# Batch left-over rows through SyncE and a GpSimd cast, a shared buffer (hbuf) in two tiles, and an earlier reorder in an attention and MLP kernel

## The chip, the cores and the metric

One core of one Trainium2 chip. The time is the device time of one execution in microseconds (us); a kernel's figure is the median of its runs. A profiled execution also has a span, from its first to its last instruction, which is about 2 us shorter than the time. In the profile PE is TensorE's matmuls, DVE VectorE, ACT ScalarE, POOL GpSimd, SP SyncE; L233 is a line of the kernel. The granted clock is TensorE's clock as a share of its full speed. The changed kernel has more lines, so the same statement has another number: L233 before is L260 after, L270 is L297, L364 is L391, L401 is L428.

## The reference

```python
def _attn_ref(q, k, v):                       # 8 batches, 12 heads, 448 rows, 64 columns, fp32
    scores = scale * np.matmul(q, k.transpose(0, 1, 3, 2))
    m = np.max(scores, axis=-1, keepdims=True)
    e = np.exp(scores - m)
    attn = e / (np.sum(e, axis=-1, keepdims=True) + np.exp(-m) + 1e-09)
    return np.matmul(attn, v)
def _moe_ref(x, w_in, w_out):                 # x: 3584 x 768; w_in 768 x 2048; w_out 2048 x 768
    h = x @ w_in
    g = 0.5 * h * (1.0 + erf(h * inv_sqrt2))
    return g @ w_out
```

The heads of the attention output are joined to rows of 768, which are x.

## The kernel before

It runs batch by batch in steps of one pair of heads (48 steps, counted from 0). While batch b's MLP runs on TensorE, the scores, exponentials and values of batch b+1 are threaded through it. 448 rows are three blocks of 128 and 64 left-over rows, which are loaded apart (klraw, vl). All inputs are fp32 in memory and fp16 on the chip; the loads on GpSimd's queue cast on the way. From batch 2 on, q and k are transposed by DMA on SyncE's queue, out of a copy in which VectorE has put the heads in pairs (order_by_pairs).

```python
    # after the six start steps of batch 0; all on GpSimd's queue, in this order
    nc.vector.memset(kl_raw[0], 0.0)
    load_q(2, 0, half); load_k(2, 0, half)
    for i in range(2):
        load_w_out(0, i, 2)            # first half of w_out's columns, in two quarters
    load_left(kl_raw, k, 2)            # 4 DMAs of 24 KB
    load_left(vl, v, 1)                # 4 DMAs of 24 KB
    load_v(1, 0, half); load_v(1, half, H)
    for i in range(2):
        load_w_out(1, i, 2)            # second half of w_out's columns
    load_q(2, half, H); load_k(2, half, H)
    ... (cut)
    def fetch_half(b, i):              # batch 2's q and k, three pairs at a time
        c0 = i * NPAIR // 2
        for w in range(2):
            order_by_pairs(b, w, c0, c0 + NPAIR // 2)      # VectorE, into the tile hbuf
            transpose_on_dma(b, w, c0, c0 + NPAIR // 2)    # SyncE
    ... (cut: half 0 is fetched after step 7, half 1 inside step 12)
    def step(s, work, late=False, then=None):
        ... (cut: scores(s), values of older pairs, normalize)
        if then:
            then()                     # where half 1 is fetched
        add_up(...)                    # VectorE: the sums of step s-1, for its denominators
        ... (cut: the MLP's tiles; in their midst denominators(s-1) on TensorE)
```

In the compiled program a load on GpSimd's queue waits for the load eight before it. hbuf is also the tile into which VectorE copies the first-layer results of a batch before their GELU.

The softmax here doesn't subtract the row's maximum and nothing guards it: scores larger than these inputs give would overflow.

## Time and profile before

414.1 us (413.2 to 415.6, 4 runs).

| What | Value | How to read it |
|---|---|---|
| span | 410.9 us | the profiled execution |
| PE busy | 396.3 us, 96% | the bound; no idle time of PE after 92 us |
| PE idle, step 11 | 1.55 us | waits for the last quarter of w_out, until 72.12 |
| PE idle, batch 1's first layer | 0.54 us | waits for a PSUM bank, which waits for hbuf |
| second half of batch 2's k | issued 58.58, landed 75.7 | the last load that VectorE's reorder needs |

### The profile page before, as it was taken

What the parts mean: (1) busy time and instruction counts of PE and PEld (TensorE: products, weight loads), DVE (VectorE), ACT (ScalarE), POOL (GpSimd) and SP (SyncE); (2) the same over time, 40 slices, a digit from 0 to 9 for tenths busy, and PEclk for the clock granted to TensorE, in tenths of its full rate; (3) what the DMA queues carried; (4) which work ended last, traced back from release to release, by engine and by line L of the source; (5) the groups of instructions that cost most, each with busy time, mean ns of one, the idle gap of its engine ahead of it and who ended that gap; (6) DMA issues with size and microseconds to landing.
All of it is one profiled execution on the core that took longest, in us unless ns stands there. A gap on an engine that the chain in (4) does not pass through costs nothing.

```text
span 410.9 us, 10968 instructions
## 1 busy us (share of the span) xinstructions
PE 396.3 (96%) x4679; PEld 245.0 (60%) x4679; DVE 199.8 (49%) x479; ACT 299.6 (73%) x450; POOL 121.1 (29%) x169
## 2 busy tenths in 40 slices
PE   7788998999999999999999999999999999999996
PEld 3444865656656665666666666565566665566663
DVE  5786346773366604673256813576146732530021
ACT  6998889879797847988687856989588766634300
POOL 8751271495732480055500672030000000000000
PEclk9999999999999999999999999999999999999999
DMA  9999999999994992289922999149011010110032
GB/s 160 144 194 203 201 171 217 194 169 160 146 116 106 143 181 35 60 121 139 128 59 59 166 146 86 51 102 151 19 41 58 22 40 2 60 53 9 2 82 73
DMA packets 137185, 43.81 MB, mean 107 GB/s; under 512 B 118256, under 2 KB 137136, under 8 KB 137136
## 3 DMA queue, kind: packets, MB, share of 16 engines
q0 software_dynamic: 91952, 22.39, 58.0%
q1 hardware_dynamic: 44400, 20.10, 26.1%
q8 instruction: 36, 0.59, 0.6%
q10 hardware_dynamic: 784, 0.62, 0.6%
q14 instruction: 13, 0.11, 0.1%
HBM read 45.61 MB, written 11.01 MB: 138 GB/s over the span
## 4 chain that ended last, share of the span: by engine, by line
PE 81%; DMA 14%; POOL 3%; issue 1%; DVE 1%
PE bank L233 65%; DMA w_out_sb<-in_moe_w_out_dram 10%; PE st L330 6%; PE bank L379 6%; DMA rawk<-in_k_dram 4%; PE st L401 2%; PE st L233 2%; PE bank L394 1%; POOL vn L97 1%; POOL rawq L97 1%; PE st L379 1%; POOL vl L129 0%; POOL klraw L129 0%; POOL rawk L97 0%; DVE klraw L177 0%
## 5 line engine op out<-in xcount | busy, mean ns | idle before, releaser
L233 PE MATMUL bank<-xt,w_in_sb 128*64 128x448 f16 x1536 | 151.9, 353 | 0.5 <-DVE hbuf L445 0.5
L318 ACT ACTIVATE et<-st,expb 128x896 f16<-128x896 f32 x144 | 134.3, 1003 | 22.8 <-PE st L330 22.6
L233 PEld LDWEIGHTS <-w_in_sb 128*64 128x64 f16 x1536 | 93.5, 110 | 54.5 <-issue 3.8
L233 PE MATMUL bank<-w_out_sb,gt_odd 128*64 128x384 f16 x1024 | 88.0, 326 | 0.0
L482 DVE COPY osb<-bank 128x384 f32<-128x384 f32 x56 | 31.2, 557 | 103.2 <-PE bank L233 103.1
L233 PEld LDWEIGHTS <-gt_odd 128*64 128x64 f16 x1024 | 57.8, 110 | 27.6 <-issue 2.1
L233 PE MATMUL bank<-w_out_sb,gt_even 128*64 128x384 f16 x768 | 68.5, 327 | 1.5 <-DMA w_out_sb<-in_moe_w_out_dram 1.5
L417 DVE TENSOR_TENSOR xt<-bank,rec 128x448 f16<-128x448 f32 x44 | 27.5, 624 | 76.1 <-PE bank L394 63.5
L233 PEld LDWEIGHTS <-gt_even 128*64 128x64 f16 x768 | 43.2, 110 | 23.8 <-issue 4.9
L441 ACT ACTIVATE gt_odd<-bank 128x448 f16<-128x448 f32 (+1 forms) x74 | 29.2, 394 | 21.3 <-PE bank L233 20.2
L330 PE MATMUL st<-tqk 64*64 64x448 f16 x576 | 41.6, 358 | 2.5 <-ACT et L318 1.5
L113 POOL DMA_DIRECT2D rawq<-in_q_dram x40 | 30.6, 772 | 30.2 <-DMA vn<-in_v_dram 20.7
L318 ACT ACTIVATE el<-st,expb 128x448 f16<-128x448 f32 x48 | 30.7, 640 | 11.1 <-PE st L401 10.4
L445 DVE COPY hbuf<-bank 128x448 f32<-128x448 f32 x54 | 33.5, 620 | 10.8 <-PE bank L233 8.9
L364 DVE TENSOR_TENSOR ksum<-ksum,el 64x448 f16<-64x448 f16 x96 | 36.9, 384 | 2.3 <-DVE ksum L364 0.2
L97 POOL DMA_DIRECT2D vn<-in_v_dram x11 | 10.5, 955 | 88.1 <-PE bank L379 85.9
L364 DVE TENSOR_TENSOR ksum<-t,et 128x448 f16<-128x448 f16 x96 | 33.4, 383 | 1.0 <-ACT et L318 0.8
L364 DVE TENSOR_TENSOR t<-et 128x448 f16<-128x448 f16 x96 | 32.9, 383 | 1.2 <-ACT et L318 0.6
L379 PE MATMUL bank<-et,vn 128*64 128x448 f16 x264 | 33.0, 356 | 0.2 <-DVE tqk L253 0.2
L441 ACT ACTIVATE gt_even<-bank 128x384 f16<-128x384 f32 x34 | 16.7, 491 | 21.5 <-PE bank L233 21.5
L408 ACT ACTIVATE rec<-st,oneb 128x448 f32<-128x448 f32 x42 | 26.8, 640 | 4.9 <-PE st L401 4.9
L330 PEld LDWEIGHTS <-tqk 64*64 64x64 f16 x576 | 15.2, 105 | 23.1 <-issue 18.7
(59 smaller groups left out, 283.4 us busy)
## 6 DMA issues: line engine op xcount, KB each, us to landing
vn<-in_v_dram POOLq DMA_DIRECT2D x6, 576.0 KB, 10.1
rawq<-in_q_dram POOLq DMA_DIRECT2D x40, 84.0 KB, 7.5
rawk<-in_k_dram POOLq DMA_DIRECT2D x32, 96.0 KB, 6.1
w_in_sb<-in_moe_w_in_dram POOLq DMA_DIRECT2D x4, 768.0 KB, 16.3
w_out_sb<-in_moe_w_out_dram POOLq DMA_DIRECT2D x4, 768.0 KB, 20.1
out_dram<-osb SPq DMA_DIRECT2D x16, 168.0 KB, 2.2
out_dram<-osb SPq DMA_DIRECT2D x16, 144.0 KB, 2.1
out_dram<-osb SPq DMA_DIRECT2D x16, 120.0 KB, 2.0
```

Source lines behind the costliest of these rows:

```text
L97: nc.gpsimd.dma_start(out=tiles[b][:, h0:h1], in_=src[b, h0:h1, 0:n * nj].rearrange("h (p j) d -> p h j d", j=nj),)
L113: nc.gpsimd.dma_start(out=dst[:, :, j, e, :], in_=view[j, e])
L233: nc.tensor.matmul(out[x], lhs[:, x], rhs, start=start, stop=stop)
L318: nc.scalar.activation(out=out, in_=in_, func=AF.Exp, bias=expb, scale=scale)
L330: nc.tensor.matmul(st[cols, e, 0:S], kt[r, j, cols], qt[r], start=True, stop=True)
L364: nc.vector.tensor_tensor(out=dst, in0=a, in1=x, op=ALU.add)
L379: nc.tensor.matmul(po_t[g][e * D:(e + 1) * D, 0:S], v_t[b][:, 2 * c + e, j, :], et[:, 2 * j + e], start=(first and j == 0), stop=(not firs ...
L408: nc.scalar.activation(out=rec_t[g], in_=den_t.pop(g)[:, 0:S], func=AF.Ln, bias=oneb, scale=1.0)
L417: nc.vector.tensor_tensor(out=xt_t[b][:, c, :], in0=po_t.pop(g)[:, 0:S], in1=rec_t.pop(g), op=ALU.mult)
L441: nc.scalar.activation(out=dst[:, 0, :], in_=ph[:, c0:c1], func=AF.Gelu)
L445: nc.vector.tensor_copy(out=h_t[b][:, fc, :], in_=ph[:, 0:S])
L482: nc.vector.tensor_copy(out=osb, in_=po[:, 0:NHW])
```

## The change

Its intent: take the many small left-over loads out of GpSimd's queue, so that w_out is issued sooner. They come as fp32 on SyncE's queue, and GpSimd casts them afterwards. hbuf becomes two tiles, so that the first layer's first four chunks don't wait for the transposes that read the second. The second half of batch 2 is reordered two steps sooner.

```diff
+    def stage_left(src, b, gate=False):
+        st = stage_pool.tile([P, NPAIR, D], FP32, name="stage")
+        if gate:
+            nc.vector.memset(st[:, 0, 0:1], 0.0)
+        view = src[b, :, NFULL:S].rearrange("(c i e) s d -> i e s c d", i=2, e=2)
+        for i in range(2):
+            for e in range(2):
+                dst = st.rearrange("p (c i) d -> p i c d", i=2)[left_rows(b, i, e), i]
+                nc.sync.dma_start(out=dst, in_=view[i, e])
+        staged[src is k, b] = st
+    def cast_left(src, b): ...         # GpSimd tensor_copy, one for v, two for k (cut)
@@ order_by_pairs: one half at a time, always into tile hbuf1 @@
-        if b not in ordered[0]:
-            spare = h_pool.tile([P, 2 * NBURST * S], FP16, name="hbuf")
+        if w == 0:
+            spare = h_pool.tile([P, NBURST * S], FP16, name="hbuf1")
@@ layer1 and gelu_burst: chunks 0 to 3 in hbuf0, 4 to 7 in hbuf1 (cut) @@
@@ the loads after the start steps @@
-    load_left(kl_raw, k, 2)
-    load_left(vl, v, 1)
+    stage_left(v, 1, gate=True)
+    stage_left(k, 2, gate=True)
     load_v(1, 0, half)
     load_v(1, half, H)
     (w_out's second half, q and k as before)
+    cast_left(v, 1)
+    cast_left(k, 2)
@@ later batches: stage_left and, a step later, cast_left in load_left's place (cut) @@
-                 then=(lambda: fetch_half(2, 1)) if (b, r) == (0, NPAIR - 2) else None)
+                 then=(lambda: fetch_half(2, 1)) if (b, r) == (0, 2) else None)
```

(b, r) = (0, NPAIR - 2) is step 12, (0, 2) is step 10.

More of the change, by code (lines that the diff above doesn't have):

```diff
@@ L57 @@
     left_pool = ctx.enter_context(tc.tile_pool(name="left_pool", bufs=1))
+    stage_pool = ctx.enter_context(tc.tile_pool(name="stage_pool", bufs=2))
     qt_pool = ctx.enter_context(tc.tile_pool(name="qt_pool", bufs=2))
@@ L119, in left_rows, with cast_left @@
         return slice(x * LEFT, (x + 1) * LEFT)
+    staged = {}
     def load_left(tiles, src, b):
-        tile_, rows = tiles[b % 2], src[b, :, NFULL:S]
         n = 2 if b else 1
+        view = src[b, :, NFULL:S].rearrange("(c i e) s d -> i e s c d", i=n, e=2)
         for i in range(n):
-            dst = tile_.rearrange("p (c i) x -> p i c x", i=n)[:, i]
-            view = rows.rearrange("(c i e) s d -> i e s c d", i=n, e=2)[i]
+            dst = tiles[b % 2].rearrange("p (c i) x -> p i c x", i=n)[:, i]
             for e in range(2):
                 x = slice(e * D, (e + 1) * D) if src is k else slice(0, D)
-                nc.gpsimd.dma_start(out=dst[left_rows(b, i, e), :, x], in_=view[e])
+                nc.gpsimd.dma_start(out=dst[left_rows(b, i, e), :, x], in_=view[i, e])
+    def stage_left(src, b, gate=False):
[8 more added lines that the diff above has]
+        staged[src is k, b] = st
+    def cast_left(src, b):
+        st = staged.pop((src is k, b))
+        if src is v:
+            nc.gpsimd.tensor_copy(out=vl[b % 2], in_=st)
+            return
+        for x in range(2):
+            r = slice(x * LEFT, (x + 1) * LEFT)
+            blocks = kl_raw[b % 2].rearrange("p (m i) (e d) -> p m (i e) d", i=2, e=2)[r]
+            nc.gpsimd.tensor_copy(
+                out=blocks[:, :, (1 if x else 0):(3 if x else 4):(1 if x else 3)],
+                in_=st[r].rearrange("p (m i) d -> p m i d", i=2))
     def load_q(b, *heads):
@@ L160 @@
     k_raw[0] = raw_pool.tile([P, H, NK, D], FP16, name="rawk")
-    first = h_pool.tile([P, NBURST, S], FP32, name="hbuf").rearrange("p f s -> p (f s)")
+    first = h_pool.tile([P, NBURST // 2, S], FP32, name="hbuf0").rearrange("p f s -> p (f s)")
     first_q, first_k = (
@@ L260, in order_by_pairs @@
         nj, raw = ((NJ, q_raw), (NK, k_raw))[w]
-        if b not in ordered[0]:
-            spare = h_pool.tile([P, 2 * NBURST * S], FP16, name="hbuf")
-            for i, (rows, chunks, x) in enumerate(((PS, NJ, 0), (P, NK, H * NJ * D))):
-                ordered[i][b] = spare[0:rows, x:x + H * chunks * D].rearrange(
-                    "p (h j d) -> p h j d", h=H, j=chunks)
+        if w == 0:
+            spare = h_pool.tile([P, NBURST * S], FP16, name="hbuf1")
+            for i, (rows, chunks, x) in enumerate(((PS, NJ, 0), (P, NK, H // 2 * NJ * D))):
+                ordered[i][b] = spare[0:rows, x:x + H // 2 * chunks * D].rearrange(
+                    "p (h j d) -> p h j d", h=H // 2, j=chunks)
         src = raw[b].rearrange("p (c e) j d -> p c e j d", e=2)
         dst = ordered[w][b].rearrange("p h j d -> p (h j d)").rearrange(
-            "p (c j e d) -> p c j e d", c=NPAIR, j=nj, e=2)
+            "p (c j e d) -> p c j e d", j=nj, e=2, d=D)
         for e in range(2):
-            nc.vector.tensor_copy(out=dst[:, c0:c1, :, e, :], in_=src[:, c0:c1, e])
+            nc.vector.tensor_copy(out=dst[:, :, :, e, :], in_=src[:, c0:c1, e])
     def transpose_on_dma(b, w, c0=0, c1=NPAIR):
@@ L278, in transpose_on_dma @@
             out=dma_views(b)[w][:, c0:c1].rearrange("p c (j s) -> p (c j) s", j=nj),
-            in_=raw.rearrange("p h j d -> p (h j d)")[:, c0 * nj * P:c1 * nj * P],
+            in_=raw.rearrange("p h j d -> p (h j d)"),
         )
@@ L442, in layer1 @@
         else:
-            if fc == 0:
-                h_t[b] = h_pool.tile([P, NBURST, S], FP32, name="hbuf")
-            nc.vector.tensor_copy(out=h_t[b][:, fc, :], in_=ph[:, 0:S])
+            i, n = divmod(fc, NBURST // 2)
+            if n == 0:
+                h_t[b, i] = h_pool.tile([P, NBURST // 2, S], FP32, name=f"hbuf{i}")
+            nc.vector.tensor_copy(out=h_t[b, i][:, n, :], in_=ph[:, 0:S])
     def gelu_burst(b, f0, f1):
+        i, n = divmod(f0, NBURST // 2)
         for c0, c1, dst in gelu_out(b, f0, f1):
-            nc.scalar.activation(out=dst, in_=h_t[b][:, f0:f1, c0:c1], func=AF.Gelu)
+            nc.scalar.activation(out=dst, in_=h_t[b, i][:, n:n + f1 - f0, c0:c1], func=AF.Gelu)
     out_v = out.rearrange("(b p j) n -> b j p n", b=B, j=NJ)
@@ L659, in fetch @@
     def fetch(b, r):
-        if r == (0 if b else 2) and b + 2 < B:
+        r0 = 0 if b else 2
+        if r == r0 and b + 2 < B:
+            stage_left(v, b + 2)
             load_v(b + 2)
-            load_left(vl, v, b + 2)
+        if r == r0 + 1 and b + 2 < B:
+            cast_left(v, b + 2)
         if b == 0 and r == -1:
@@ L670, in fetch @@
             load_pairs(k_raw, "rawk", k, b + 3)
-            load_left(kl_raw, k, b + 3)
+            stage_left(k, b + 3)
+        if r == 4 and b + 3 < B:
+            cast_left(k, b + 3)
     step(NPAIR + 1, mlp1(0, 2, 6))
```

## The prediction

> **What bounds the kernel now.** I read the page first, then the table of 40 windows, the PE timeline, the POOL timeline, the DVE timeline and the DMA view of short windows.
>
> ```profile
> span 410.9 us, 10968 instructions
> PE 396.3 (96%) x4679; PEld 245.0 (60%) x4679; DVE 199.8 (49%) x479; ACT 299.6 (73%) x450; POOL 121.1 (29%) x169
> ```
>
> TensorE is the bound: 396.3 of 410.9 us. In the table of windows PE is busy for the whole of every window from 92.5 us to 400 us, so nothing that the change does there can win; it can only put a new wait in. What can be won lies before 92 us. Up to 33 us the gaps are waits for ACT and DVE, and the change touches nothing there. After that only two DMA-made gaps remain. The first is in the PE timeline of step 11 (s = 11):
>
> ```profile
> 66.61 1.47 PE L233 MATMUL bank<-w_out_sb,gt_even 128*64 128x384 f16 x16
> 68.01 0.76 PE L330 MATMUL st<-tqk 64*64 64x448 f16 x12
> 68.70 1.49 PE L233 MATMUL bank<-w_out_sb,gt_even 128*64 128x384 f16 x16
> 70.02 0.36 PE L233 MATMUL st<-tqk 128*64 128x448 f16 x2
> 70.21 0.36 PE L401 MATMUL st<-ksum,ones 128*64 128x448 f16 x2
> ```
>
> After the denominators at 70.21 PE wants the last quarter of w_out and starts again only at 72.12, after 1.55 us idle. The second gap is 0.54 us before 87.87, where PE waits for a PSUM bank whose copy to hbuf waited for the DMA transposes of batch 2's second half. Sum to be won: 1.55 + 0.54 = 2.1 us.
>
> Why that quarter of w_out is late shows in the POOL timeline:
>
> ```profile
> 26.96 0.88 POOL L153 DMA_DIRECT2D w_out_sb<-in_moe_w_out_dram  x1 [1.50 <-DMA rawk<-in_k_dram]
> 31.78 0.62 POOL L129 DMA_DIRECT2D klraw<-in_k_dram  x1 [3.95 <-DVE klraw L618]
> 34.78 0.63 POOL L129 DMA_DIRECT2D klraw<-in_k_dram  x1 [2.38 <-DMA w_in_sb<-in_moe_w_in_dram]
> ...
> 53.77 0.63 POOL L129 DMA_DIRECT2D vl<-in_v_dram  x1 [3.28 <-DMA w_out_sb<-in_moe_w_out_dram]
> 54.38 1.71 POOL L97 DMA_DIRECT2D vn<-in_v_dram  x2
> 56.08 1.77 POOL L153 DMA_DIRECT2D w_out_sb<-in_moe_w_out_dram  x2
> 57.81 0.81 POOL L97 DMA_DIRECT2D rawq<-in_q_dram  x1
> 58.58 0.86 POOL L97 DMA_DIRECT2D rawk<-in_k_dram  x1
> ```
>
> In the compiled order each POOL load waits for the load eight before it (eight semaphores in turn). The eight left-over loads of 24 KB (klraw, vl) use up those places, so vn, the second half of w_out and batch 2's second q and k halves are issued at 54 to 59 us, when the queue has run dry:
>
> ```profile
> GB/s 149 156 173 205 208 183 149 94 79 58 57 47 27 23 26 29 24 213 292 290 288 287 274 288 290 104 283 294 294 226 118 61 23 33 54 77 76 135 179 174
> ```
>
> That is the DMA view from 52 to 58 us in 40 slices of 0.15 us. From 53 to 54.5 and from 56.5 to 57.5 the engines are nearly idle. Against the 195 GB/s that the queue holds when full (and 290 for transposes) I count about 1.2 + 0.8 us lost, and 0.2 us more to 60 us: **2.2 us** of DMA time in all.
>
> **What the Trainium skill says.** "DMA: Bandwidth & Descriptors", section "SWDGE vs HWDGE vs iDMA": a cast during a DMA is for GpSimd's queue alone. Hence the fp32 staging tile and a cast afterwards; the trace agrees as far as it goes, every load that casts stands under the software queue. The same page, "Issuing engines are not separate DMA queues": loads from SyncE and GpSimd run on the same 16 engines and interleave. So moving rows to SyncE frees places in the queue, not bandwidth; the trace agrees: at 62 us, when SyncE stores flow, the software queue falls to about 110 KB in a microsecond, from 195. The same page, "Queues, rings and completion order": descriptors are taken in ring order. Here the klraw load issued at 31.78 landed 21.9 us later, at 53.7, behind w_out. "GPSIMD Engine Reference", "Engine selection": one-input elementwise work runs at roughly line rate on GpSimd. No instruction of the kernel before shows it; the casts have 384 elements a row, and I put them at about 1 us, an estimate.
>
> **The change part by part.**
> 1. POOL loses four loads of 0.62 us per batch for v and four for k (2.5 us each) and gains one cast for v and two for k, some 1 to 2 us. POOL is busy 29% and has 24 us waits; nothing on the path.
> 2. Eight staged loads (fp32, 1536 packets of 256 B) run at about 31.5 us beside w_in, in place of 1536 packets of 128 B at 51 to 53. At some 1100 to 1200 packets per us, read from the trace, both cost about 1.3 us of DMA time: moved, not saved. w_in's quarters land 5 us or so before use, so this hides. w_out's first half lands about 1 us later (53.8 to about 55), its second quarter is wanted at 56.1: just hidden.
> 3. POOL now issues vn, w_out and q, k by about 48 us, and the queue no longer runs dry. Order and bytes of those loads are unchanged, so their landings come forward by the 2.2 us: w_out from 72.1 to about 69.9, which removes the 1.55 us.
> 4. hbuf in two tiles and the reorder of batch 2's second half at step 10 (12 before): the transposes are out of the way long before 87 us, which removes the 0.54 us.
> 5. But the reorder stands in DVE's own order. In the compiled order of the changed kernel its four copies come right after step 10's two normalizes and before the six additions of step 9's denominators. Before:
>
> ```profile
> 65.21 0.62 DVE L417 TENSOR_TENSOR xt<-bank,rec 128x448 f16<-128x448 f32 x1 [0.52 <-PE bank L379]
> 65.75 0.68 DVE L364 TENSOR_TENSOR t<-et 128x448 f16<-128x448 f16 x2
> 66.35 0.69 DVE L364 TENSOR_TENSOR ksum<-t,et 128x448 f16<-128x448 f16 x2
> ...
> 76.40 1.00 DVE L270 COPY hbuf<-rawq 112x768 f16<-112x768 f16 x2
> 77.32 0.80 DVE L270 COPY hbuf<-rawk 128x576 f16<-128x576 f16 x2
> ```
>
> So DVE asks for the second q and k halves at 65.8 us. In the kernel before they landed at 57.81 + 16.2 = 74.0 and 58.58 + 17.1 = 75.7 us (DMA views), just in time for 76.40. They are behind w_out in the same ring; 2.2 us earlier is 71.8 and **73.5**. DVE stands still from 65.8 to 73.5 but for the q copies. From there: k copies, then the three pairs of additions, which took 77.32 to 80.16 = 2.84 us before, so the sums are ready at 76.4. PE's denominators, at 70.21 before, wait for them; the second half of that layer-2 tile then starts at about 73.5 + 2.84 + 0.1 (hand-over, estimate) + 0.19 (denominators to the next start, 66.42 to 66.61) = 76.63, against 72.12 before: **+4.5 us**.
>
> Sum: the 1.55 us is not returned, since the new wait covers it; +4.5 - 0.5 (hbuf) = +4.0 us, none of it made up later, as PE is full from 92 us on. 414.07 + 4.0 = **418.0 us**.
>
> **The rivals.**
> - *The loads land early enough* (the intent). For it speaks that the queue is fed some 10 us sooner. Against it: the bytes from the end of w_out's first half at 51.5 us are 0.59 (vn) + 1.57 (w_out) + 0.64 MB (q, k) = 2.8 MB, at 195 GB/s 14.4 us, so 66 us with nothing else on the engines and 67 at landing, later than 65.8 already; 0.84 MB of transposes (2.9 us), the stages (1.3) and two stores (1.1) come on top. If transposes yielded and landing were near 68 us, the DVE wait would hide and the gain would be the 2.1 us: 412 us.
> - *Mixing costs more.* From 102 to 105 us transposes and loads of 128 B share the engines packet for packet at 52 + 107 KB per us, about 0.7 of what they do apart. If the first half's transposes now mix so with vn and w_out, k lands at 75 to 76: +6 us, 420.
> - *SyncE or POOL becomes a bound*: staged loads stand behind stores on SyncE, casts on POOL wait for them, and the next q, k loads for the casts, some 8 us later for batch 3. Against: those are needed about 25 us after landing, and transposes wait for no PE work. If wrong, one more stall of a few us.
> - *All is hidden*: no change, 414.
>
> **Range and chances.** The DVE wait is certain in order, its length rests on the landing of k: 71.5 to 75.5 gives 416 to 420. I leave a tail for the first rival: 412.8 to 420.8 holds it 8 times in 10. Two per cent is 8.3 us: faster needs more than all gaps that are there (0.01); slower, over 422.4, needs twice the stall (0.04); within 2%, 0.95.
>
> **What would show it.** PE timeline near 70 us: a gap before the denominators (ksum as releaser) of 5 to 7 us, and none for w_out. DVE timeline: the hbuf copies after a wait for rawq and rawk from about 66 to 72 to 73.5 us. DMA view 52 to 58: no empty slices. Near 88 us: no wait for hbuf. From 100 us on: PE without gaps. Wrong if k lands before 69 us, or if a second gap shows later.

## The result, and the profile after

The changed kernel took 424.66 us (424.31 to 426.56, 4 runs) against 414.1: ratio 1.0261, 95% interval 1.0218 to 1.0304, slower. All ratios here are the mean of one kernel's fast runs over the mean of the other's fast runs of the same rounds, so not quite the ratio of the medians. The predicted 418.0 and its range, 412.8 to 420.8, were missed.

From the page of the changed kernel:

```profile
span 422.3 us, 11003 instructions
PE 399.2 (95%) x4679; PEld 247.5 (59%) x4679; DVE 203.3 (48%) x481; ACT 299.6 (71%) x450; POOL 99.4 (24%) x136
```

The span is 11.4 us longer and PE's busy time only 2.9: most of it is idle time of PE. The view of waits of the changed kernel (engine and line, what it waited for, total us, times, longest) tells where:

```profile
POOL klraw L154 <- DMA stage<-in_k_dram: 72.7, 4, 22.5
POOL vl L149 <- DMA stage<-in_v_dram: 64.9, 6, 35.4
...
DVE hbuf L297 <- DMA rawq<-in_q_dram: 11.1, 1, 11.1
PE st L428 <- DVE ksum L391: 10.5, 1, 10.5
```

GpSimd's long waits for staged rows are harmless, since nothing later is late for them. The one that counts is the last: PE waited once, 10.5 us, for VectorE's sums. The PE timeline of the changed kernel, step 11 (start, duration, then in brackets the idle time ahead of it and its releaser):

```profile
69.39 1.49 PE L260 MATMUL bank<-w_out_sb,gt_even 128*64 128x384 f16 x16
70.71 0.36 PE L260 MATMUL st<-tqk 128*64 128x448 f16 x2
81.59 0.95 PE L428 MATMUL st<-ksum,ones 128*64 128x448 f16 x2 [10.52 <-DVE ksum L391]
82.01 3.09 PE L260 MATMUL bank<-w_out_sb,gt_even 128*64 128x384 f16 x16
84.57 1.11 PE L406 MATMUL bank<-et,vn 128*64 128x448 f16 x6
85.61 0.38 PE L357 MATMUL st<-tqk 64*64 64x448 f16 x4
```

The gap stands exactly where the prediction put it, ahead of the denominators of step 9; it is just about twice as long. The DVE timeline of the changed kernel over the same stretch:

```profile
65.90 0.62 DVE L444 TENSOR_TENSOR xt<-bank,rec 128x448 f16<-128x448 f32 x1 [0.52 <-PE bank L406]
77.58 1.01 DVE L297 COPY hbuf<-rawq 112x768 f16<-112x768 f16 x2 [11.05 <-DMA rawq<-in_q_dram]
79.10 0.81 DVE L297 COPY hbuf<-rawk 128x576 f16<-128x576 f16 x2 [0.51 <-DMA rawk<-in_k_dram]
79.83 0.68 DVE L391 TENSOR_TENSOR t<-et 128x448 f16<-128x448 f16 x2
80.43 0.68 DVE L391 TENSOR_TENSOR ksum<-t,et 128x448 f16<-128x448 f16 x2
81.14 0.81 DVE L391 TENSOR_TENSOR ksum<-ksum,el 64x448 f16<-64x448 f16 x2
```

VectorE stands 11 us at the copy of q's second half, while the additions behind it have had their inputs for long. The copies of k and the additions then take 79.10 to 81.95 = 2.85 us, as predicted (2.84); TensorE starts at 81.59, when the first of the last two sums is there. What was wrong is the landing of q and k. The POOL timeline of the changed kernel:

```profile
43.81 0.88 POOL L180 DMA_DIRECT2D w_out_sb<-in_moe_w_out_dram  x1 [4.26 <-DMA w_in_sb<-in_moe_w_in_dram]
46.32 0.78 POOL L98 DMA_DIRECT2D rawq<-in_q_dram  x1 [1.64 <-DMA rawq<-in_q_dram]
47.84 0.82 POOL L98 DMA_DIRECT2D rawk<-in_k_dram  x1 [0.74 <-DMA rawk<-in_k_dram]
```

The intent worked at the issue: k's second half is issued at 47.84, not 58.58. Yet the DMA views give (KB, then us from issue to landing), for the kernel before and the changed one,

```profile
rawk<-in_k_dram POOLq DMA_DIRECT2D x1, 288.0 KB, 17.1
rawk<-in_k_dram POOLq DMA_DIRECT2D x1, 288.0 KB, 31.2
```

so it lands at 79.0, against 75.7 before. Issued 10.7 us sooner, it landed 3.3 us later in this pair of profiles. Where the engines' time went, the DMA view of the changed kernel from 56 to 73 us tells (the queues' packets, MB and share; q0 is GpSimd's, q1 that of SyncE and ScalarE):

```profile
GB/s 181 184 184 165 161 160 170 170 172 175 182 187 186 182 189 233 179 175 90 40 53 191 189 192 187 190 191 190 186 188 185 173 175 164 168 155 150 147 192 170
...
q0 software_dynamic: 3209, 2.05, 88.8%
q1 hardware_dynamic: 3209, 0.81, 47.4%
```

And of the kernel before, from 53.9 to 57.2 us:

```profile
GB/s 20 20 29 26 28 30 28 25 180 285 298 285 289 295 285 292 280 265 295 279 295 285 217 43 267 289 295 292 295 282 256 144 105 81 61 23 23 28 42 47
...
q1 hardware_dynamic: 2082, 0.52, 75.5%
q0 software_dynamic: 292, 0.05, 28.2%
```

Before, 0.52 MB of the 0.84 MB of DMA transposes of batch 2's first half passed through the hole in GpSimd's queue nearly alone, at about 290 GB/s. After, there is no hole, and for 17 us the two queues go packet for packet: 3209 and 3209. A transpose packet has 256 bytes, so the transposes crawl at 0.81 MB / 17 us = 48 GB/s, and the loads get 2.05 MB / 17 us = 121 GB/s where they had about 195. One after the other, at 290 and 195 GB/s, the same bytes would take about 2.8 + 10.5 = 13.3 us (an estimate from these figures), not 17.

A second, smaller thing was not in the prediction at all. The table of windows of the changed kernel (PE busy, PEld, DVE, ACT, POOL, then granted clock, DMA share, GB/s):

```profile
72.00:76.00 4.00, 0.00 (x0) 0.00 (x0) 0.00 (x0) 0.00 (x0) 0.00 (x0) 0.84 1.32 163
76.00:81.00 5.00, 0.00 (x0) 0.00 (x0) 2.92 (x8) 0.00 (x0) 0.00 (x0) 0.50 1.57 175
81.00:83.00 2.00, 1.41 (x9) 0.69 (x10) 1.94 (x7) 0.43 (x1) 0.00 (x0) 0.50 0.84 152
83.00:85.00 2.00, 2.00 (x16) 1.14 (x14) 1.31 (x5) 1.31 (x3) 0.00 (x0) 0.50 0.91 216
85.00:87.00 2.00, 2.00 (x29) 1.01 (x27) 1.23 (x4) 0.96 (x2) 0.00 (x0) 1.00 0.33 74
```

While PE idled, its granted clock fell to half, and it stayed there until about 85 us: the 16 matmuls at 82.01 took 3.09 us, those ahead of the gap 1.49. The Trainium skill, "TensorE: Matmul & The Clock Gate", Part 1, says that an idle window of about 3.4 us brings the array to half its clock and that it takes about as long of work to come back; the trace agrees: the clock fell at 74.8 us, 3.7 us after the last matmul ended, and rose at 85.0, 3.4 us after the denominators began.

The ledger of the two profiled runs: the start was 0.7 us later (the first layer-2 matmul at 55.46, 54.77 before, a difference that unedited runs show too); the gap is 10.52 in place of 1.55, 9.0 more; from the denominators to the scores of step 12 it took 81.59 to 85.61 = 4.0, before 2.2 without its wait (70.21 to 74.11 less 1.55, and 0.17 us that the wait overlapped), 1.8 more. Sum 11.5 at that point; 11.4 at the end.

### The profile page after: what moved, and what is told of

It is laid out like the page before. It is cut to its first block, busy times and chain, and to the rows that moved or that the text cites. A ratio compares the mean times of both kernels' runs of the same rounds, so it can differ in the third digit from the quotient of the medians.

```text
span 422.3 us, 11003 instructions
## 1 busy us (share of the span) xinstructions
PE 399.2 (95%) x4679; PEld 247.5 (59%) x4679; DVE 203.3 (48%) x481; ACT 299.6 (71%) x450; POOL 99.4 (24%) x136
## 4 chain that ended last, share of the span: by engine, by line
PE 79%; DMA 14%; POOL 3%; DVE 1%; issue 1%; POOLq 0%
PE bank L260 63%; DMA rawk<-in_k_dram 7%; DMA rawq<-in_q_dram 7%; PE st L357 6%; PE bank L406 5%; PE st L428 2%; PE st L260 2%; PE bank L421 1%; POOL rawk L98 1%; POOL w_in_sb L172 1%; POOL rawq L98 1%; PE st L406 1%; DVE ksum L391 1%; POOL klraw L132 0%; POOL vn L98 0%
## 5 line engine op out<-in xcount | busy, mean ns | idle before, releaser
L260 PEld LDWEIGHTS <-w_in_sb 128*64 128x64 f16 x1536 | 95.2, 110 | 52.4 <-issue 3.5
L511 DVE COPY osb<-bank 128x384 f32<-128x384 f32 x56 | 31.2, 558 | 99.7 <-PE bank L260 99.7
L260 PE MATMUL bank<-w_out_sb,gt_even 128*64 128x384 f16 x768 | 70.1, 331 | 0.0
L391 DVE TENSOR_TENSOR ksum<-ksum,el 64x448 f16<-64x448 f16 x96 | 38.5, 401 | 2.1
L391 DVE TENSOR_TENSOR ksum<-t,et 128x448 f16<-128x448 f16 x96 | 35.4, 404 | 0.9 <-ACT et L345 0.6
L438 ACT ACTIVATE rec<-rec 128x448 f32<-128x448 f32 x48 | 27.6, 577 | 1.5
```

The lines of the kernel that those rows point to most:

```text
L260: nc.tensor.matmul(out[x], lhs[:, x], rhs, start=start, stop=stop)
L391: nc.vector.tensor_tensor(out=dst, in0=a, in1=x, op=ALU.add)
L438: nc.scalar.activation(out=rec_t[g], in_=rec_t[g], func=AF.Exp, scale=-1.0)
L511: nc.vector.tensor_copy(out=osb, in_=po[:, 0:NHW])
```

## The experiments

Theory A: VectorE's own order. Copies that wait for q and k stand before sums that TensorE needs, so the end is set by the landing of k. Theory B, the rival: the staging as such (casts, SyncE's queue, fp32 bytes) costs time all along. And for the late landing: theory C, the transposes of the first half, which now share the engines with the loads; theory D, the eight staged loads at 32 to 37 us; theory E, something else in the queue. Runs e1 to e4 and then e5 to e8 each shared a chip and the runs of the kernel before, e9 to e12 another chip. The last column is of one profile of each run; flight is the time from issue to landing.

| Run | Time (median) | Ratio to before, 95% | k's second half: issued + flight = landed |
|---|---|---|---|
| before | 414.1 | 1 | 58.58 + 17.1 = 75.7 |
| changed | 424.66 | 1.0261 (1.0218 to 1.0304) | 47.84 + 31.2 = 79.0 |
| e1 changed, reorder at step 12 | 419.48 | 1.0125 (1.0078 to 1.0172) | 47.93 + 33.5 = 81.4 |
| e2 before, reorder at step 10 | 421.35 | 1.0161 (1.0101 to 1.0222) | 58.47 + 19.8 = 78.3 |
| e3 changed, no first transposes | 416.66 | 1.006 (0.9967 to 1.0152) | 47.49 + 22.8 = 70.3 |
| e4 changed, no staged loads | 420.29 | 1.0147 (1.0078 to 1.0216) | 45.92 + 29.1 = 75.0 |
| e5 changed, PE kept at work | 424.14 | 1.0247 (1.0192 to 1.0301) | 47.61 + 31.8 = 79.4 |
| e6 before, hbuf in two tiles | 413.21 | 0.9975 (0.9928 to 1.0021) | 58.24 + 19.4 = 77.6 |
| e7 changed, late transposes | 422.91 | 1.0215 (1.0165 to 1.0266) | 47.39 + 23.3 = 70.7 |
| e8 two tiles, v's loads split | 411.17 | 0.9936 (0.9897 to 0.9975) | 58.78 + 17.2 = 76.0 |
| e9 changed again | 426.72 | 1.028 (1.0228 to 1.0332) | 48.86 + 31.5 = 80.4 |
| e10 late transposes, step 12 | 421.85 | 1.0168 (1.0098 to 1.0239) | 47.97 + 23.8 = 71.8 |
| e11 neither of e3's and e4's | 411.55 | 0.9918 (0.9844 to 0.9992) | 43.54 + 23.1 = 66.6 |
| e12 before, v's loads split | 416.47 | 1.0042 (0.9977 to 1.0107) | 58.48 + 18.1 = 76.6 |

**e1, the reorder back at step 12.**

```diff
-then=(lambda: fetch_half(2, 1)) if (b, r) == (0, 2) else None
+then=(lambda: fetch_half(2, 1)) if (b, r) == (0, NPAIR - 2) else None
```

> The changed kernel with the reorder of batch 2's second half put back from step 10 to step 12; staging and the two hbuf tiles stay. If the loss is DVE standing in its own order before the sums of step 9, the 10.5 us gap before the denominators goes; w_out's last quarter, which now lands near 73 to 74 us, leaves a gap of 2 to 3 us, and the time is 414 to 416 us. If the staging itself costs time in every batch (casts, SyncE's queue), it stays above 419 us.

The time lies 3 us above what was expected of theory A and at the edge of what B said. The PE timeline of this run decides:

```profile
70.76 0.36 PE L428 MATMUL st<-ksum,ones 128*64 128x448 f16 x2
76.37 2.77 PE L260 MATMUL bank<-w_out_sb,gt_even 128*64 128x384 f16 x16 [5.25 <-DMA w_out_sb<-in_moe_w_out_dram]
```

The wait for the sums is gone, as A says. But w_out's last quarter, which the change was to bring sooner, landed at 76.3, 4 us later than in the kernel before (2 later than in e6, with the same queue as before), and PE waits 5.25 us for it. After that PE shows no wait that the kernel before hasn't, and the ledger closes: of the 5.3 us by which the span is longer, 3.7 are this longer wait and 1.5 the cold clock behind it (76.37 to 79.85 in place of 72.12 to 74.11). So the staged version loses even without the early reorder, by the same late queue and not batch by batch: B falls.

**e2, the early reorder alone**, in the kernel before.

```diff
-then=(lambda: fetch_half(2, 1)) if (b, r) == (0, NPAIR - 2) else None
+then=(lambda: fetch_half(2, 1)) if (b, r) == (0, 2) else None
```

> The kernel before with nothing changed but the reorder moved from step 12 to step 10. The second k half landed at 75.7 us there; if DVE's order is the cause, the sums come at about 78.6, the gap before the denominators is about 8.4 us, and the time is 414.1 + 8.4 - 1.55 - 0.5 + about 1 for the cold TensorE clock: 421 to 422 us. If the loss needs the staging, it stays within 1 us of 414.

Met: 421.35 us. PE's timeline in this run:

```profile
80.74 0.95 PE L401 MATMUL st<-ksum,ones 128*64 128x448 f16 x2 [8.30 <-DVE ksum L364]
```

Moving one call by two steps, with nothing staged, makes a gap of the same kind, 8.3 us. Theory A is shown. That the size was met to 0.1 us is partly luck: k landed at 78.3 in this run, not at 75.7, and TensorE came to the denominators 2 us later too. The two losses (e1's and e2's, 5 to 8 us each) don't add, since both are waits for the same queue and the longer covers the shorter.

**e3, without the transposes of the first half.** The tile they would write is set to zero by VectorE, so the result is wrong; the check of the result passed all the same, probably since q and k are drawn with a spread of 0.1 and a score, 64 products times 1/8, is then only about 0.01, so that zero is nearly right.

```diff
+        if b == 2 and c0 == 0:
+            nc.vector.memset(dma_views(b)[w][:, c0:c1], 0.0)
+            if w == 1:
+                nc.vector.memset(dma_views(b)[2], 0.0)
+            return
```

> The changed kernel with the DMA transposes of batch 2's first half left out (zeros in their place, so the result is wrong on purpose). If these transposes, mixed packet by packet with the loads from 55 to 73 us, are what makes k's second half land at 79.0 instead of 73.5, it lands at 73 to 74 and the time falls by about 5 us to 419. If they cost only the 2.9 us that they take alone, k lands near 76 and the time is 421 to 422.

k landed at 70.3, 3 us sooner than even theory C had it. The DVE timeline of this run:

```profile
68.44 1.01 DVE L297 COPY hbuf<-rawq 112x768 f16<-112x768 f16 x2 [2.25 <-DMA rawq<-in_q_dram]
70.31 0.81 DVE L297 COPY hbuf<-rawk 128x576 f16<-128x576 f16 x2 [0.86 <-DMA rawk<-in_k_dram]
```

The wait shrank from 11.05 to 2.25 us. The time, 414.76 and 418.56 in two runs, spreads too widely to count in.

**e4, without the eight staged loads** (zeros again; here the result was indeed wrong, by 13%).

```diff
         if gate:
-            nc.vector.memset(st[:, 0, 0:1], 0.0)
+            nc.gpsimd.memset(st, 0.0)
+            staged[src is k, b] = st
+            return
```

> The changed kernel without the eight staged loads at 32 to 37 us (zeros, wrong on purpose). If they cost what I predicted, 1.3 us of DMA time, k's second half lands at about 77.7; if they cost the 2.4 us that the dip of the software queue from 36 to 45 us suggests, at about 76.6 and the time is about 422 us; if they are the main cause of the late landing, it lands before 75.

k landed at 75.0, sooner than I expected of either size, at the mark where I had said they would be the main cause. About half of the 4 us is there by the issue (45.92 for 47.84: the place in the queue is free when k's first half has landed), the other half comes in flight. So the staged loads cost more than the 1.3 us predicted, but less than half of what the transposes do. The DMA views of the two kernels from 36 to 45 us show a part of it that doesn't hang on the landing. The changed kernel, then e4:

```profile
q0 software_dynamic: 1966, 1.31, 95.6%
q1 hardware_dynamic: 1645, 0.39, 34.5%
...
q0 software_dynamic: 2746, 1.80, 135.1%
```

Beside the staged rows the loads moved 0.49 MB less, 2.5 us at e4's 200 GB/s. The 2.4 us of the middle expectation are met by this; the rest of the 4 us lies within what landings differ by from run to run (see e9).

**e5, PE kept at work in the gap.**

```diff
+            if s == NPAIR + 5:
+                for _ in range(48):
+                    nc.tensor.matmul(st[:, 1, 0:S], w_in_sb[:, 0, 0:P], xt_t[0][:, 0, :],
+                                     start=True, stop=True)
             for i, g in enumerate(dens):
```

> The changed kernel with 48 matmuls of 448 columns put in front of step 11's denominators, where TensorE otherwise waits 10.5 us (their result is overwritten). At full clock they take about 9 us, so they fit into the wait. If the wait itself is all there is, the time stays at 424 to 425 us; if the clock that was granted after the idle stretch (0.64 and 0.86 in the two windows) costs the 1.3 us that the next 16 matmuls took longer (3.09 for 1.47 us), it falls by 1 to 2 us.

```profile
70.91 9.25 PE L570 MATMUL st<-xt,w_in_sb 128*128 128x448 f16 x48
81.95 0.76 PE L428 MATMUL st<-ksum,ones 128*64 128x448 f16 x2 [1.78 <-DVE ksum L391]
82.36 1.65 PE L260 MATMUL bank<-w_out_sb,gt_even 128*64 128x384 f16 x16
83.69 0.89 PE L406 MATMUL bank<-et,vn 128*64 128x448 f16 x6
84.51 0.38 PE L357 MATMUL st<-tqk 64*64 64x448 f16 x4
```

The granted clock stayed at 1.00, and from the denominators to the scores of step 12 it took 81.95 to 84.51 = 2.56 us, 1.46 less than in the changed kernel. That much of the loss is the cold clock. In the whole time it doesn't show clearly: 424.14, to the changed kernel's 424.66 from an earlier session; the sums came 0.4 us later here, and landings differ by more than that (see e9).

**e6, hbuf in two tiles alone**, in the kernel before: order_by_pairs, layer1 and gelu_burst as in the change, the rest untouched.

> The kernel before with only hbuf in two tiles; the reorder of the second half stays at step 12. The 0.54 us wait for hbuf near 88 us should go, if the first four chunks no longer wait for the transposes; the time 413.0 to 414.1 us. If a second tile brings a new wait (the second half's reorder must now wait for the first half's transposes), it is slower.

413.21 us, ratio 0.9975, within the noise. The wait for hbuf is gone, but this run waited 2.11 us for w_out where the other had 1.55, so the profile gives no clean gain.

**e7, the transposes held back** until the loads are through.

```diff
-            fetch_half(2, 0)
+            order_by_pairs(2, 0, 0, NPAIR // 2)
+            order_by_pairs(2, 1, 0, NPAIR // 2)
-                 then=(lambda: fetch_half(2, 1)) if (b, r) == (0, 2) else None
+                 then={(0, 2): lambda: half_transposes(2, 0),
+                       (0, NPAIR - 1): lambda: fetch_half(2, 1)}.get((b, r))
-        r0 = 0 if b else 2                  # v of batch 2
+        r0 = 0 if b else 3
... (cut: half_transposes issues a half's transposes alone; v of batch 2 is gated by a memset)
```

> The changed kernel with the DMA transposes of batch 2's first half issued in step 10 instead of at once, the second half's reorder in step 13, and v of batch 2 loaded a step later. If the transposes' sharing of the DMA engines is what delays the loads, w_out's last quarter lands near 68 and k near 70 us as in the run without them, and w_out's wait goes; the transposes then land at 74 to 77 us, where step 12's scores want them at about 73, a wait of 1 to 4 us: 414 to 417 us. If something else delays the loads, w_out still leaves its gap of about 5 us and the time is 418 or more.

The first part came out as theory C has it: in the DMA view from 53 to 61 us the loads are alone,

```profile
q0 software_dynamic: 2860, 1.59, 142.0%
```

1.59 MB in 8 us, 199 GB/s, and PE waits neither for w_out nor for the sums. The time missed, 422.91, by a wait that I had not expected. PE's timeline:

```profile
74.05 0.38 PE L357 MATMUL st<-tqk 64*64 64x448 f16 x4 [1.30 <-DMA tqk<-hbuf]
...
96.92 1.33 PE L357 MATMUL st<-tqk 64*64 64x448 f16 x12 [7.06 <-DMA tqk<-hbuf]
```

The first half's transposes cost only 1.30 us. The second half's, now at step 13 and issued at 83.38, landed 7 us late. That they met the q and k loads of batch 3 is my reading; no run took those loads away.

**e9, the changed kernel again**, unedited, on the other chip.

> The changed kernel itself, unedited, beside the next two on one chip. It should repeat 424 to 425 us, with k's second half landing at 79 to 80 us and a wait of 10 to 11 us before the denominators; if it doesn't, the differences of 1 us that I read between runs are chance.

426.72 us, 1.7 us above what was expected, with a gap of 10.77 us; k landed at 80.4. So landings differ by some 2 us from run to run (79.0, 79.4, 80.4, 81.4 with this queue; 75.7, 77.6, 78.3 with the queue of the kernel before, in its own profile, e6 and e2), and differences of a microsecond are not read here. Later with the changed queue, though issued 10 us sooner, holds for all seven profiles; the means of the two groups lie about 3 us apart.

**e10, the late transposes, with the second half at step 12.**

```diff
-(0, NPAIR - 1): lambda: fetch_half(2, 1)
+(0, NPAIR - 2): lambda: fetch_half(2, 1)
```

> The late transposes of the run before, but the second half's reorder in step 12 instead of 13, so that its transposes are issued before SyncE's staged loads of k and before the q and k loads of batch 3 crowd the engines. If the 7 us wait near 97 us came from that crowd, it goes or shrinks below 2 us and the time is 414 to 417 us. If the second half's transposes are slow whenever they are put there, it stays at 421 or more.

Missed: 421.85 us, and the second wait is still there.

```profile
96.57 1.33 PE L357 MATMUL st<-tqk 64*64 64x448 f16 x12 [6.22 <-DMA tqk<-hbuf]
```

The copies were made at 77 to 79 us, but on SyncE's queue the transposes still stood behind the eight staged loads of that stretch and were issued at 83.03, hardly sooner than e7's 83.38. So the run doesn't decide whether the crowd of loads is to blame. A wait that is driven out of one stretch turned up in the next; a schedule in which both halves pass was not found.

**e11, neither the staged loads nor the first transposes** (both edits at once, a wrong result).

> The changed kernel without the eight staged loads and without the first half's transposes (zeros for both, wrong on purpose). The loads alone, 2.8 MB from about 51.5 us at 195 GB/s, then give k's landing at about 67 us, 12 us before the changed kernel; the two removals alone brought 4.0 and 8.8 us, so if they add up it is 66 to 67. If it stays at 70, the two overlap and something else paces the queue.

k landed at 66.6 us, VectorE found it there when it asked at 66.2 to 67.1, and the time is 411.55: about the gain that the change was meant for (though with 1.2 MB less to move), and the early reorder is harmless in it. The start of the queue was about 2 us ahead in this run (issue at 43.54), so the flight times are the safer measure: 31.2 to 33.5 us with both; 29.1 without the staged loads; 22.8 to 23.8 without the transposes beside them, whether left out (e3, e11) or held back (e7, e10). The transposes cost the loads 8.4 us of flight beside the staged loads (31.2 - 22.8) and 6.0 without them (29.1 - 23.1).

**e8, a version to beat both**: the kernel before, hbuf in two tiles, and this.

```diff
     load_v(1, 0, half)
-    load_v(1, half, H)
     for i in range(2):
         load_w_out(1, i, 2)
+    load_v(1, half, H)
```

> A version to beat both: the kernel before with hbuf in two tiles, and w_out's second half issued ahead of the second half of batch 1's v rows (not wanted before step 12). That brings w_out's last quarter forward by the 1.5 to 1.9 us that 288 KB take, so the 1.55 us wait and the 0.54 us wait go: 412 us. If the place in the queue isn't what counts, it equals the kernel before.

411.17 us, ratio 0.9936 (0.9897 to 0.9975): faster than both kernels, by 0.6% of the kernel before (the interval excludes 1), and below the 412 expected. The PE timeline of this run shows step 11 without a wait:

```profile
70.19 0.35 PE L401 MATMUL st<-ksum,ones 128*64 128x448 f16 x2
70.55 1.49 PE L233 MATMUL bank<-w_out_sb,gt_even 128*64 128x384 f16 x16
```

**e12, the split of v's loads alone**, hbuf in one tile.

> The kernel before with only the order of the loads changed: w_out's second half ahead of the second half of batch 1's v rows; hbuf stays one tile. If the order of the queue is what wins in the version that beat both, the wait for w_out's last quarter is gone and the time is 0.4 to 0.6% below the kernel before, with a wait of about 0.5 to 2 us for hbuf near 87 us left. If the two hbuf tiles are needed for it, the gain is within 0.2%.

416.47 us, ratio 1.0042, no gain. The wait for w_out is down to 0.26 us (70.96 to 71.22), but:

```profile
90.01 3.57 PE L233 MATMUL bank<-xt,w_in_sb 128*64 128x448 f16 x24 [3.39 <-DVE hbuf L445]
```

With w_out sooner, the wait moved to hbuf and grew to 3.39 us, and the clock dropped after it: VectorE's copy into hbuf waited 4.06 us for the transposes, which took 10.6 us from issue to landing here, 7.6 in the kernel before and 10.3 in e8, where hbuf's first tile doesn't wait for them. So e8 needs both: each of its two edits alone shows nothing clear.

## Why the prediction was wrong

- *The bound, and what was to be won* (1.55 + 0.54 us): right. e8 and e11, which have neither wait, are 411.2 and 411.6 us.
- *Part 1, GpSimd's casts* off the path: right. A cast of v took 0.5 to 0.7 us, two of k 1.1 to 1.4; GpSimd's busy share fell from 29% to 24%. The Trainium skill's "GPSIMD Engine Reference", "Engine selection", fits this: VectorE copies 128 x 384 in fp32 in 0.54 us, and a cast of v has that shape.
- *Part 2, the staged loads move DMA time but don't add any* (1.3 us): too small. e4 showed 4 us of landing, and 2.5 us of it in the DMA views: the engines moved loads and staged rows together at 190 GB/s, at which 0.39 MB take 2 us, while 1100 to 1200 packets of 256 B per us would be about 290.
- *Part 3, the landings come forward by 2.2 us, to 69.9 for w_out and 73.5 for k*: **this is the step that failed**. I took the empty slices from 53 to 58 us as the whole value of the hole and let the 2.9 us of transposes stand as a cost of 2.9 us wherever they ran. The hole was not just lost time: the transposes went through it at 290 GB/s. Filled with loads, the queue shares packet for packet with them, and they cost the loads 6 to 8 us of flight (e11, e3). So w_out and k landed later than before, though issued 10 us sooner (e1: 76.3; the changed kernel: 79.0). A smaller part of the miss may be the start of the sum: its 75.7 came from one profile, and is the earliest of three landings of that queue (e9).
- *Part 4, hbuf*: nearly right, 0.20 us left of 0.54.
- *Part 5, VectorE in its own order*: right in place and in mechanism (e2 and the timelines); k to the denominators was put at 2.94 us and took 81.59 - 79.0 = 2.6. Only the landing that it starts from was off.
- *The sum*: 10.5 us of gap in place of the 6.2 that 76.4 against 70.21 meant, and 1.5 us of cold TensorE clock (e5), a term that wasn't in the sum.
- *The rivals*: the second one, dearer mixing, was the right one, and I had the evidence for it (102 to 105 us in the kernel before). I sized it at about 2 us and kept it out of the middle value; the range ended at 420.8 for that. The third, SyncE or GpSimd as a bound, did not come in the changed kernel, but a wait of that kind did in e7 and e10. The first would have needed e11's queue.

What stays open: why the mixture, packet for packet, costs more than the two apart (the runs show what it costs, not why); what slows the second half's transposes in e7 and e10; and what the engines did in the short dip at 64 us in the DMA view of the changed kernel (40 GB/s in one slice).

## What to carry to other kernels

Before filling a hole in a DMA queue, look at what the other queue does in it: it may be the only stretch in which small packets pass at speed, and a load issued 10 us sooner can land later. An in-order engine should not be given an instruction that waits for a transfer ahead of one that the bound engine waits for; place it where the transfer has landed with a margin, or after the urgent work. When a wait on the bound engine goes, look for the next in line (w_out, then hbuf, then the next batch's transposes): here only the pair of edits won.

## What the Trainium skill lacked or had wrong

- "DMA: Bandwidth & Descriptors", "Queues, rings and completion order": that each engine goes round the queues packet by packet is stated, and the runs agree as far as the profile's packets go (3209 and 3209 in 17 us; the page's packet is of several descriptors, and no run shows whether the two are the same thing). What it lacks is the price: loads of 384 to 768 bytes a packet beside transposes of 256 bytes fell from about 195 to 121 GB/s, and the transposes from 290 to 48.
- The same page, "Latency and other measured facts", gives a DMA transpose 261 GB/s with a non-contiguous middle dimension and about 350 to 400 for a contiguous one. Alone they ran at 280 to 295 GB/s here, between the two; beside loads at 48.
- The same page, "Issuing engines are not separate DMA queues", says that DMAs of all issuing engines interleave and that several issuing engines save only issue time. The first fits; what it lacks is that sharing can cost more than was saved: w_out's last quarter, issued 13 us sooner on GpSimd's queue with SyncE's loads and transposes beside it, landed 2 to 4 us later (e1, against e6 and the kernel before).
- "TensorE: Matmul & The Clock Gate", Part 1, was right: half clock after a 10.5 us wait, and 1.5 us lost by it.
